# Halved modulation columns, two-group k projections, a split last output tile and a re-made order in a one-core adaLN, Hedgehog attention and MLP-mixer kernel

## The chip, the cores and the metric

The kernel runs on one core of one Trainium2 chip. The metric is the device time of one execution in microseconds (us). Three runs of the kernel before gave 551.48, 550.83 and 550.70 us, with a median of 550.83 us. One further execution was taken by the hardware profiler. It took 551.07 us, of which the span from the first instruction to the last is 549.2 us, so 1.87 us lie around the span.

## The reference, cut to what matters

The input is one sequence of 2048 rows and 512 features. A condition vector `c` gives six modulation rows, of which the change touches the first two (`sa` and `ca`).

```python
mod = (silu(c) @ w_mod).reshape(1, 6, 1, -1)
sa, ca, ga, sb, cb, gb = (mod[:, i] for i in range(6))
h = layernorm(x) * (1 + ca) + sa
x = x + ga * A(h)          # Hedgehog linear attention, 32 heads of 16
h = layernorm(x) * (1 + cb) + sb
x = x + gb * B(h)          # spatial shift mixer, then an MLP of width 1376

# A: q, k, v = h @ wqkv ; pq, pk = q @ w_phi, k @ w_phi (per head)
#    phi = concat(softmax(p), softmax(-p)) ; kv = phi_k^T v ; z = sum(phi_k)
#    o = (phi_q kv) / (phi_q z + 1e-6) ; A = o @ wo
# B: x1 = x + shift(gelu(layernorm(x) @ w1)) @ w2
#    B = x1 + gelu(layernorm(x1) @ w3) @ w4
```

## The kernel before, in words

The 2048 rows are 16 tiles of 128 rows, in 8 chunks of two tiles. Nearly every product is made of three fp32r matmuls (high and low parts of both operands), which `three` lists.

**The start.** `load_folded` multiplies the k weight (and later the q weight) by the block-diagonal `w_phi`: four groups of four matmuls each, tile names `bd`, `rk` in and `pp` out, split into high and low parts `w` by ScalarE and VectorE. `mod_cols` (L526) makes the first two modulation rows as columns. Four loads of 512 KB, one for each 128 rows of `w_mod`, bring the `sa` and `ca` columns of all 512 features. Four groups of matmuls add into one PSUM tile (32 partitions for each quarter). A copy `mod`, two transposes and two small additions then make the columns `const`. `h_chunk` turns the normalised tiles (`xn`) by transposes into `pt`, scales them with the columns, and splits them into `hh`, in two halves of two feature blocks each.

**The first pass.** For each chunk, `k_feat` and `q_feat` make the projections of k and q (12 matmuls of 512 columns in a tile `pp`), and VectorE, ScalarE and GpSimd do the two softmaxes on tiles `ke` and `qe`. `v_feat` makes v, and `kv_add` sums the products into `kva`. `zacc` sums the k features on VectorE or GpSimd. The last tile's features are not added there. They are added by matmuls (`BIAS["zpe"]`), which wait for the `ke` of tile 15.

**The later passes.** `phase_a` makes the attention output and the mixer. `up` and `down_steps` make the MLP in seven Strassen-like products of halves. `down_steps` sums each chunk of two tiles in four PSUM tiles `ac` (called `acc[0]` to `acc[3]`). `finish_rows` adds them to the residual rows `xb` by way of `uu`, and stores the result. For the last chunk, each tile's sum is added and stored in two halves of 256 columns.

**What sets the order.** Nothing is issued where it is written. Every operation is recorded in a `Plan`, and the table `ORDER` at the top of the file lists the numbers of the operations in the sequence in which they are emitted. A letter behind a number (A, V or G) moves an operation to ScalarE, VectorE or GpSimd where it has that choice. The table `SLOT` says which buffer, or which of the 8 PSUM banks, each tile uses. Each engine then runs its own instructions strictly in that order, and waits for what they need. All loads and stores go through SyncE (SP), except two small loads by ScalarE (L449). The helpers record everything, so that L468 is every matmul, L477 every transpose, L398 and L407 the copies and scalings, L415 and L417 additions on VectorE and GpSimd, L439 reductions, L445 loads and L452 stores.

Of the kernel before, what the change touches and what calls it, by code (L numbers as in the profile page):

```python
# [160 lines left out]
)  # L161
SLOT = {
    "pp": "2112103775712644371760105367611260725752737061505556300230174572340654633645407076250504027663340302"
          "145552521507",
    "bd": "13",
    "w": "174625cd387165ad28cb09",
    "rk2": "5846",
    "x2": "9",
    "st": "1377h22bbb1155hh02hg88gbf79d90221",
    "mv": "0bh0e42j01f3f380d28hebh03dg0bc0bb",  # L170
# [1251 lines left out]
```

## Time and profile before

| What | Value |
|---|---|
| Median of three runs | 550.83 us |
| Profiled execution | 551.07 us |
| Span of the profiled execution | 549.2 us |
| TensorE busy (PE) | 541.0 us, 98% |
| VectorE busy (DVE) | 492.2 us, 90% |
| GpSimd busy (POOL) | 372.7 us, 68% |
| ScalarE busy (ACT) | 339.8 us, 62% |
| Mean granted TensorE clock | 0.998 |

PE is the matmuls and PEld the weight loads that run beside them. A row of the timeline gives the start in us from the span's start, the duration in us, the engine, the line, the operation, the tiles written and read, the shape, the count, and in brackets how long the engine was idle before and what ended that. A "q" behind an engine marks its queue, which issues transfers. A row of the DMA view ends with the KB of one transfer and the us from its issue to its landing.

### The profile page before, as it was taken

What the parts mean: (1) busy time and instruction counts of PE and PEld (TensorE: products, weight loads), DVE (VectorE), ACT (ScalarE), POOL (GpSimd) and SP (SyncE); (2) the same over time, 40 slices, a digit from 0 to 9 for tenths busy, and PEclk for the clock granted to TensorE, in tenths of its full rate; (3) what the DMA queues carried; (4) which work ended last, traced back from release to release, by engine and by line L of the source; (5) the groups of instructions that cost most, each with busy time, mean ns of one, the idle gap of its engine ahead of it and who ended that gap; (6) DMA issues with size and microseconds to landing.
All of it is one profiled execution on the core that took longest, in us unless ns stands there. A gap on an engine that the chain in (4) does not pass through costs nothing.

```text
span 549.2 us, 12264 instructions
## 1 busy us (share of the span) xinstructions
PE 541.0 (98%) x4474; PEld 484.0 (88%) x4474; DVE 492.2 (90%) x899; ACT 339.8 (62%) x800; POOL 372.7 (68%) x383
## 2 busy tenths in 40 slices
PE   7999999999999999999999999999999999999997
PEld 6888788888677887888889999999999999999996
DVE  4999999999999999999998988988889768988887
ACT  2799988734436896959898576873533535234430
POOL 2388988979599999998995264433655653355354
PEclk9999999999999999999999999999999999999999
DMA  8975364247485669886898899989469746592032
GB/s 320 350 242 211 109 186 157 77 140 235 135 225 183 194 205 296 253 271 233 234 309 315 274 351 328 361 329 326 192 184 389 245 174 237 191 356 87 1 117 76
DMA packets 63668, 124.89 MB, mean 227 GB/s; under 512 B 7060, under 2 KB 26772, under 8 KB 59512
## 3 DMA queue, kind: packets, MB, share of 16 engines
q1 hardware_dynamic: 63320, 124.04, 66.4%
q8 instruction: 35, 0.57, 0.5%
q14 instruction: 25, 0.20, 0.1%
q10 hardware_dynamic: 288, 0.07, 0.1%
HBM read 89.74 MB, written 34.35 MB: 226 GB/s over the span
## 4 chain that ended last, share of the span: by engine, by line
PE 84%; DVE 9%; DMA 2%; issue 2%; POOL 2%; ACT 1%; DVEq 0%; POOLq 0%
PE pp L468 32%; PE pa L468 28%; PE ac L468 20%; PE pt L477 3%; DVE q L439 2%; DMA mod<-in_wmod 1%; DVE k L439 1%; DVE pz L439 1%; DVE pT L688 1%; DVE ke L415 1%; DMA const<-in_c 1%; DVE qe L415 1%; POOL qe L417 1%; PE kva L468 1%; ACT n L398 0%
## 5 line engine op out<-in xcount | busy, mean ns | idle before, releaser
L468 PE MATMUL pp<-w,hh 128*128 128x512 f32 x576 | 138.2, 397 | 0.0
L468 PEld LDWEIGHTS pp<-w,hh 128*128 128x128 f32 x576 | 106.8, 188 | 25.3 <-issue 1.0
L468 PE MATMUL pa<-bH,wq 128*128 128x256 f32 x840 | 105.9, 281 | 0.0
L468 PE MATMUL ac<-w,gg 128*128 128x256 f32 x840 | 105.4, 281 | 0.0
L468 PEld LDWEIGHTS ac<-w,gg 128*128 128x128 f32 x840 | 102.9, 188 | 1.2
L468 PEld LDWEIGHTS pa<-bH,wq 128*128 128x128 f32 x840 | 102.7, 188 | 0.6
L417 POOL TENSOR_TENSOR gg<-cu,gg 128x128 fp32r<-128x128 f32 (+1 forms) x32 | 21.4, 675 | 40.7 <-PE ac L468 13.8
L468 PE MATMUL pp<-w,sh 128*128 128x512 f32 x192 | 47.9, 397 | 0.0
L468 PE MATMUL pp<-w,oT 128*128 128x512 f32 x192 | 47.1, 395 | 0.0
L468 PE MATMUL pa<-nT,w 128*128 128x256 f32 x384 | 46.2, 279 | 0.0
L468 PEld LDWEIGHTS pa<-nT,w 128*128 128x128 f32 x384 | 45.1, 188 | 0.9 <-ACT mv L592 0.2
L468 PEld LDWEIGHTS pp<-w,sh 128*128 128x128 f32 x192 | 35.1, 188 | 8.6 <-POOL sh L1050 0.5
L468 PEld LDWEIGHTS pp<-w,oT 128*128 128x128 f32 x192 | 35.6, 188 | 8.0
L585 POOL TENSOR_TENSOR rs<-mv,const 128x2 f32<-128x2 f32 x31 | 24.3, 785 | 24.5 <-ACT mv L592 22.9
L398 ACT ACTIVATE cu<-pa 128x512 f32<-128x512 f32 (+1 forms) x41 | 21.3, 525 | 31.0 <-PE pa L468 13.6
L398 ACT ACTIVATE gg<-cu 128x256 fp32r<-128x256 f32 (+1 forms) x48 | 16.5, 360 | 25.0 <-PE ac L468 22.4
L417 POOL TENSOR_TENSOR e<-e,q 128x1024 f32<-128x1024 f32 x15 | 29.9, 2009 | 0.0
L415 DVE TENSOR_TENSOR gg<-sg,gg 128x512 fp32r<-128x512 f32 x36 | 26.3, 736 | 4.0 <-ACT gg L398 2.7
L417 POOL TENSOR_TENSOR ez<-e,const 128x1024 f32<-128x1024 f32 x12 | 28.8, 2407 | 0.1
L417 POOL TENSOR_TENSOR ke<-ke,k 128x1024 f32<-128x1024 f32 x14 | 28.6, 2049 | 0.0
L398 ACT ACTIVATE gg<-sg 128x512 fp32r<-128x512 f32 x28 | 17.3, 625 | 18.1 <-DVE gg L407 6.7
L415 DVE TENSOR_TENSOR cu<-pa,cu 128x512 f32<-128x512 f32 (+1 forms) x36 | 21.0, 594 | 7.5 <-PE pa L468 5.9
(221 smaller groups left out, 1224.7 us busy)
## 6 DMA issues: line engine op xcount, KB each, us to landing
wq<-dram SPq DMA_DIRECT2D x32, 1024.0 KB, 7.3
dram<-ws SPq DMA_DIRECT2D x35, 256.0 KB, 3.9
dram<-qe SPq DMA_DIRECT2D x16, 512.0 KB, 3.5
e<-dram SPq DMA_DIRECT2D x64, 128.0 KB, 3.6
xl<-in_x SPq DMA_DIRECT2D x30, 256.0 KB, 3.9
raw<-in_w SPq DMA_DIRECT2D x18, 256.0 KB, 4.0
mod<-in_wmod SPq DMA_DIRECT2D x16, 256.0 KB, 4.9
dram<-xl SPq DMA_DIRECT2D x16, 256.0 KB, 3.8
```

What stands on the lines that cost most here:

```text
L398: nc.scalar.activation(o(), i(), func, **kw)
L415: dve = ("DVE", 71 + 1.04 * o.n + 90 * (isps(a) and isps(b)), lambda: nc.vector.tensor_tensor(o(), a(), b(), op=op))
L417: pool = ("Pool", cost, lambda: nc.gpsimd.tensor_tensor(o(), a(), b(), op=op))
L439: plan.op("DVE", 65 + 1.04 * a.n + 110 * isps(o), lambda: nc.vector.tensor_reduce(o(), a(), axis=AX.X, op=op), [o], [a])
L468: nc.tensor.matmul(o(), a(), b(), start=s, stop=e, **kw)
L477: nc.tensor.transpose(o(), i(), ident())
L585: plan.op("Pool", 540 + 10 * m, lambda: nc.gpsimd.tensor_tensor(r(), v(), mhalf[:, :m](), op=OP.pow), [r], [v, mhalf])
L688: plan.op("DVE", 71 + 1.04 * o.n, lambda: nc.vector.transpose(o(), i()), [o], [i])
```

## The change

**Columns in two parts.** `mod_cols` takes a part. Part 0 makes the columns of the first 256 features (for `sa` and `ca` together), part 1 those of the other 256. The host lays the first 1024 columns of `w_mod` out anew, so that one part's columns lie together. There are still four loads of 512 KB, now two for each part, each with two blocks of 128 rows and runs of 2 KB in place of 4 KB. A load's matmuls become 8 of 128 columns in place of 4 of 256. Each part has its own copy, one transpose, and two additions.

**k of tiles 0 and 1 in two groups.** `k_feat` of chunk 0 records its 12 matmuls as two operations of 6, the first of which needs only the first half of `hh`.

**The last tile.** For the last tile's second half, `down_steps` puts the product of the remaining 96 hidden units (tile `gl`) into a PSUM tile of its own (`apart_`), and the first half's into `acc[3]`: 6 matmuls of 256 columns in place of 3 of 512. `finish_rows` adds and stores the two halves from the two tiles. The first half's store is issued by ScalarE.

**The tables.** `ORDER` and `SLOT` are replaced as a whole. The rows of these tables tell nothing by themselves. The two halves of the table `pp` below only show the kind of thing that changes.

```diff
-    "pp": "2112103775712644371760105367611260725752737061505556300230174572340654633645407076250504027663340302"
+    "pp": "1711324063347164027171451064250123635713170533160754233252706645706753646036434077762560040275463453"
...
-    def mod_cols():
+    wide = T("const", [P, NK, 32])
+    def mod_cols(part):
-        p, r, pc = T("pp", [P, HD]), T("mod", [P, HD]), T("pp", [P, 2, P])
-        for k in range(NK):
+        if part == 0:
+            act(wide, sv[:, :, None].bc([P, NK, 32]), alts=("DVE",))
+        p, r, pc = T("pp", [P, P]), T("mod", [P, P]), T("pp", [P, P])
+        for a in range(0, NK, 2):
             raw = T("mod2", [P, 2, D])
-            load(raw, wmod_d[k * P:(k + 1) * P, :2 * D].rearrange("p (j n) -> p j n", j=2), 2 * P * D * 4)
-            mms([(p[32 * (2 * j + h):32 * (2 * j + h + 1)], wide[:, k, :], raw[:, j, h * HD:(h + 1) * HD], k == 0, k == NK - 1)
-                 for j in range(2) for h in range(2)], [p], [wide, raw], skip=True, tiles=4)
+            load(raw, wmod_d[a * P:(a + 2) * P, part * D:(part + 1) * D].rearrange("(a p) n -> p a n", a=2), 2 * P * D * 4)
+            mms([(p[32 * i:32 * (i + 1)], wide[:, a + k, :], raw[:, k, i * P:(i + 1) * P], a + k == 0, a + k == NK - 1)
+                 for k in range(2) for i in range(NK)], [p], [wide, raw], skip=True, tiles=4)
         act(r, p, alts=("DVE",))
-        transp([(pc[:, i, :], r[:, i * P:(i + 1) * P]) for i in range(2)], [pc], [r])
+        transp([(pc, r)], [pc], [r])
...
-        ks = [k_feat(hh, t, wk, c * TPC + t) for t in range(TPC)]
+        ks = [k_feat(hh, t, wk, c * TPC + t, 1 if c else 2) for t in range(TPC)]
...
+        apart_ = T("ac", [P, HD]) if c == NC - 1 else None
...
+                    if t and apart_ is not None:
+                        for o, n, whole in ((apart_, slice(HD, D), True), (acc[3][:, 0, :], slice(HD), False)):
+                            mms(three(o, g[:n9, 0, sl], g[:n9, 1, sl], last["w4"][0][:n9, n], last["w4"][1][:n9, n], whole, whole),
+                                [o], [g, *last["w4"]], skip=True)
+                        continue
...
-                tt(x1[:, a, :], x1[:, a, :], p[:, a, :], OP.add)
-                store(out[rows_, a * HD:(a + 1) * HD], x1[:, a, :], P * HD * 4)
+                tt(x1[:, a, :], x1[:, a, :], apart_ if t and a else p[:, a, :], OP.add)
+                if t and not a:
+                    plan.op("Activation", 60, lambda dst=out[rows_, :HD], i=x1[:, 0, :]: nc.scalar.dma_start(dst, i()), [], [x1[:, 0, :]],
+                            land=2400)
+                else:
+                    store(out[rows_, a * HD:(a + 1) * HD], x1[:, a, :], P * HD * 4)
```

The new tables move instructions on every engine. Three places matter for what follows: the start (on two engines), the sum of the k features, and the end. In the listings a tile's number only tells it from others of its name.

**SyncE's first loads.** This is the queue of the loads at the very start, before: `rk` are the k weights (first two) and the q weights (last two), `x` is chunk 0, `xl` are later tiles, `mod` the modulation weights.

```order
L445 DMA rk_3_69<-in_wqk_t 128x2x512
L445 DMA const_78<-in_cst 128x256
L445 DMA x_7_80<-in_x 128x2x512
L445 DMA rk_8_82<-in_wqk_t 128x2x512
L445 DMA mod_9_84<-in_wmod 128x1024
L445 DMA mod_11_91<-in_wmod 128x1024
L445 DMA mod_12_93<-in_wmod 128x1024
L445 DMA mod_14_100<-in_wmod 128x1024
L445 DMA rk_16_104<-in_wqk_t 128x2x512
L445 DMA rk_18_108<-in_wqk_t 128x2x512
L445 DMA xl_119<-in_x 128x512
```

The same queue after the change, up to the last of the two parts' loads:

```order
L445 DMA const_69<-in_cst 128x256
L445 DMA rk_5_76<-in_wqk_t 128x2x512
L445 DMA rk_6_78<-in_wqk_t 128x2x512
L445 DMA xl_80<-in_x 128x512
L445 DMA x_8_82<-in_x 128x2x512
L445 DMA rk_10_89<-in_wqk_t 128x2x512
L445 DMA xl_91<-in_x 128x512
L445 DMA rk_12_93<-in_wqk_t 128x2x512
L445 DMA mod_14_97<-in_wmod 128x2x512
L445 DMA mod_17_106<-in_wmod 128x2x512
L445 DMA mod_27_142<-in_wmod 128x2x512
L445 DMA mod_29_146<-in_wmod 128x2x512
```

The two q weight loads and two tiles of chunk 1 now stand ahead of the modulation weights.

**VectorE from the columns to the first k.** Before, the columns are the two additions into `const_224` (one row, x2), and all of `hh` follows them:

```order
L407 TENSOR_SCALAR mod_219<-pp_183 128x256
L426 TENSOR_SCALAR const_224<-pp_221 128x2x2 x2
L407 TENSOR_SCALAR pt_214<-pt_214,const_224 128x256
L407 TENSOR_SCALAR pt_202<-pt_202,const_224 128x256
L407 TENSOR_SCALAR hh_243<-pt_202 128x512
L415 TENSOR_TENSOR hh_243<-pt_214,hh_243 128x512
L415 TENSOR_TENSOR hh_243<-pt_202,hh_243 128x512
L415 TENSOR_TENSOR w_271<-pp_238,w_254 128x4x128
```

After, `const_270` is written twice, for the first 256 features and then for the others, and the two halves of `hh` lie around the second:

```order
L426 TENSOR_SCALAR const_270<-pp_261 128x2 x2
L407 TENSOR_SCALAR w_210<-pp_213 128x4x128
L415 TENSOR_TENSOR w_246<-pp_213,w_210 128x4x128
L415 TENSOR_TENSOR hh_293<-pt_263,hh_293 128x512
L426 TENSOR_SCALAR const_270<-pp_316 128x2 x2
L407 TENSOR_SCALAR pt_252<-pt_252,const_270 128x256 x2
L407 TENSOR_SCALAR hh_293<-pt_252 128x512
L415 TENSOR_TENSOR hh_293<-pt_252,hh_293 128x512
L407 TENSOR_SCALAR w_210<-pp_205 128x4x128
L415 TENSOR_TENSOR w_246<-pp_205,w_210 128x4x128
```

The folds of the q weights (`w_210`, `w_246`) moved in between. On TensorE, all eight groups of folds now stand ahead of the modulation matmuls, the eight transposes of chunk 1 stand between the two parts, and the k matmuls come behind part 1's transpose: 6 of tile 1, 12 of tile 0, and the other 6 of tile 1.

**TensorE at the sum of the k features.** Late in the first pass, two rows (`pp` from `za`, then from `ke`) sum the k features of all tiles by matmuls with ones. `ke` is tile 15, still to be finished by VectorE. Before, they stand behind 36 matmuls of 512 columns that follow a group of `kva`:

```order
L468 MATMUL pp_1756<-w_351,hh_1193 128x512
L468 MATMUL pp_1756<-w_288,hh_1193 128x512
L468 MATMUL pp_1777<-za_825,const_67 32x256 x4
L468 MATMUL pp_1777<-ke_1720,const_67 32x256 x4
L468 MATMUL pp_1796<-w_288,hh_1398 128x512
```

After, with the same `kva` group ahead:

```order
L468 MATMUL pp_1800<-w_358,hh_1374 128x512
L468 MATMUL pp_1800<-w_352,hh_1374 128x512
L468 MATMUL pp_1817<-za_856,const_67 32x256 x4
L468 MATMUL pp_1817<-ke_1704,const_67 32x256 x4
L468 MATMUL pp_1835<-w_352,hh_1374 128x512
```

Now 48 matmuls of 512 columns stand between that `kva` group and the sum: one projection of 12 has moved ahead of it.

**VectorE at the end.** These are the last instructions of VectorE before. `ac_7381`, `ac_7392`, `ac_7404` and `ac_7447` are the last chunk's `acc[0]` to `acc[3]`, `xb_6790` and `xb_7365` its two tiles of rows.

```order
L415 TENSOR_TENSOR xb_6790<-xb_6790,ac_7381 128x256
L415 TENSOR_TENSOR xb_6776<-xb_6776,ac_7279 128x512
L407 TENSOR_SCALAR uu_7500<-ac_7381 128x256
L415 TENSOR_TENSOR gg_7437<-cu_6863,gg_7363 128x256
L415 TENSOR_TENSOR uu_7500<-uu_7500,ac_7381 128x256
L415 TENSOR_TENSOR uu_7500<-uu_7500,ac_7392 128x256
L415 TENSOR_TENSOR xb_7365<-xb_7365,xc_7357 128x512
L415 TENSOR_TENSOR xb_7365<-xb_7365,ac_7392 128x256
L415 TENSOR_TENSOR uu_7500<-uu_7500,ac_7392 128x256
L415 TENSOR_TENSOR xb_6790<-xb_6790,ac_7404 128x256 x2
L415 TENSOR_TENSOR xb_7365<-xb_7365,ac_7447 128x256 x2
```

After, `acc[0]` to `acc[3]` are `ac_7447`, `ac_7398`, `ac_7418` and `ac_7549`, and `apart_` is `ac_7544`:

```order
L407 TENSOR_SCALAR uu_7510<-ac_7447 128x256
L415 TENSOR_TENSOR xb_6765<-xb_6765,ac_7315 128x512
L415 TENSOR_TENSOR uu_7510<-uu_7510,ac_7447 128x256
L415 TENSOR_TENSOR xb_7378<-xb_7378,xc_7368 128x512
L415 TENSOR_TENSOR uu_7510<-uu_7510,ac_7398 128x256
L415 TENSOR_TENSOR xb_7378<-xb_7378,ac_7398 128x256
L415 TENSOR_TENSOR uu_7510<-uu_7510,ac_7398 128x256
L415 TENSOR_TENSOR xb_6795<-xb_6795,ac_7447 128x256
L415 TENSOR_TENSOR xb_6795<-xb_6795,ac_7418 128x256 x2
L415 TENSOR_TENSOR xb_7378<-xb_7378,ac_7544 128x256
L415 TENSOR_TENSOR xb_7378<-xb_7378,ac_7549 128x256
```

The last two rows now read two tiles, and the addition of `acc[0]` to the first tile's rows moved from the first row shown to the row ahead of `ac_7418`. In the new `SLOT` table `acc[3]` has the bank of `acc[0]`, and `apart_` that of `acc[1]`; before, the four had a bank each. So the matmuls into `apart_` wait for the last read of `acc[1]`, and those into `acc[3]` for the last read of `acc[0]`.

More of the change, by code (lines that the diff above doesn't have):

```diff
@@ L40 @@
 ORDER = (
[120 rows of a table removed]
[120 rows of a table added]
 )
 SLOT = {
-    "pp": "2112103775712644371760105367611260725752737061505556300230174572340654633645407076250504027663340302"
[L164 to L170, printed above, removed]
-    "rs": "29812hcbbjji851d0ie93863874jh6213",
-    "nm": "3fa4a54dde4e1jjcf2883583gaacj278gb331h60ed7ha0092e635b5a",
-    "xn": "10cg751eba368fe9",
@@ L174 @@
-    "mod": "lh9g7ejf9i4638bkia",
-    "mod2": "0213",
+    "pp": "1711324063347164027171451064250123635713170533160754233252706645706753646036434077762560040275463453"
+          "62046562621057",
+    "bd": "2j",
+    "w": "134702cd89516a7d49c210",
+    "rk2": "4195",
+    "x2": "3",
+    "st": "201e1g254426a5555ca22555f27582006",
+    "mv": "4355172614f1f5a4hac5dic53c22cccg0",
+    "rs": "9232251141c55d5ab5a1fed21a4e82084",
+    "nm": "6402c757j74f422161488a44dd699b5jjijj2fc8b5i7fc1ehge226d2",
@@ L176 @@
+    "xn": "f083kge1k95hlici",
+    "mod": "i9805j174ejdf793i1g",
+    "mod2": "2647",
     "kva": "4",
     "za": "7",
-    "hh": "30a89be0",
-    "pt": "06254521753213317025344576360400",
-    "raw": "da1k0d63f6hg40cljd4940abi353",
-    "k1": "2430035525435132",
-    "ke": "4501639451823940",
-    "k2": "1213035252034134",
-    "vv": "ib4j953cdj19a75f",
-    "qe": "3792232883214942",
-    "q1": "2440243225135053",
-    "qt": "5e97g70fkccg",
-    "xl": "abd42002jf51cl836e2i1h3b0j5g2je53k0hhej4hlahd0",
@@ L189 @@
-    "acc": "cl8hi",
-    "kvs": "f",
-    "pz": "1",
-    "q2": "10141003",
-    "e": "5617956758034928",
-    "ez": "8348813999970750",
-    "q3": "2212223043334222",
-    "q5": "23253203",
-    "pT": "4272394975373487",
-    "oT": "99594b24",
-    "nT": "9999bb2e",
-    "n": "1931gfgfahafb63g",
-    "h": "7kd9l62c7i1lfkcd",
-    "gf": "17555662",
-    "sh": "2520ecb0",
-    "pa": "762553462761040036271541705740316243253470661263027034160772",
-    "wr": "80061",
-    "ws": "khe217da8lk4eba05bb5dfgfd71i652ak90",
@@ L207 @@
-    "gb": "8",
-    "tw": "98935",
-    "bL": "47604149",
-    "nb": "1ahb5c79egg4jc3f",
-    "yt": "e5jkbdh7j9l9a6cd",
-    "bH": "52804219431594595069127578657523",
-    "tr": "714eb039akdl4172",
-    "wq": "490c934e174e3174e7314e7134ee3417e431",
-    "cu": "672egi14f3fl25b7c10g4hg9ked6l14g9cd0jblf",
-    "gl": "c3jca56i",
-    "ac": "26311567160267423016415376013542",
-    "gg": "32781952372584716531287609873295063284107962583012103241806937415809263740821596",
-    "sg": "bkbka76k6hk6h4kj6a25j37b2lbji26k2i2594k2",
@@ L220 @@
-    "xb": "9had9ei0fc3ha71e",
-    "xc": "5lj03023672l0gfh",
-    "uu": "j3347ell",
+    "hh": "86596bea",
+    "pt": "05266253756236307563344627135340",
+    "raw": "akl5db94201k385ljd4940abi353",
+    "k1": "0231523433000413",
+    "ke": "4506239453821940",
+    "k2": "3112123212413411",
+    "vv": "bf4c218453gde20k",
+    "qe": "2798812825711992",
+    "q1": "1243144314035413",
+    "qt": "hfe58k5d0h08",
+    "xl": "k4hd6282blae03h76e2i3e5b0jjg2jeb3k0hhej9hlahd3",
+    "acc": "6c4gh",
+    "kvs": "d",
@@ new lines @@
+    "pz": "1",
+    "q2": "12313230",
+    "e": "5637986458013928",
+    "ez": "1841273373970050",
+    "q3": "0001000001142121",
+    "q5": "14233433",
+    "pT": "1553393927171752",
+    "oT": "47ee0744",
+    "nT": "ab744343",
+    "n": "fbb787g7daafb63g",
+    "h": "gkd9l62c7i1lfkcd",
+    "gf": "73510949",
+    "sh": "0abe2b2e",
+    "pa": "572553547504540036271543705740316243053470661263027010166772",
+    "wr": "10064",
+    "ws": "0j629gdfe9lab6a15fcf3fghdh1i652ak90",
+    "gb": "8",
+    "tw": "93534",
@@ new lines @@
+    "bL": "07600143",
+    "nb": "1ahb5a794eg4j5ab",
+    "yt": "eg6kbdhej9lj20cd",
+    "bH": "82865219931451257925167078517526",
+    "tr": "710ek536g42l010l",
+    "wq": "30ec03b85e5b38e5be38be583beeb583e5b8",
+    "cu": "672egi14fkfl25b7c10g4hg9ked6l14g9cd0jblf",
+    "gl": "c3jca5e5",
+    "ac": "263115671602674206354153760125325",
+    "gg": "32781452832481796237489625863492354180697320581769960241803976415809234760821593",
+    "sg": "bkb6f76keh96h4kj6a2ja37b27lji26k2i2296i2",
+    "xb": "9had9ei0fc3ha71k",
@@ L223 @@
+    "xc": "0lj030j3i42bl45f",
+    "uu": "j33jakll",
 }
@@ L524, in mod_acc @@
         return acc
-    def mod_cols():
-        wide = T("const", [P, NK, 32])
-        act(wide, sv[:, :, None].bc([P, NK, 32]), alts=("DVE",))
-        p, r, pc = T("pp", [P, HD]), T("mod", [P, HD]), T("pp", [P, 2, P])
-        for k in range(NK):
+    wide = T("const", [P, NK, 32])
[4 more added lines that the diff above has]
+        for a in range(0, NK, 2):
             raw = T("mod2", [P, 2, D])
-            load(raw, wmod_d[k * P:(k + 1) * P, :2 * D].rearrange("p (j n) -> p j n", j=2), 2 * P * D * 4)
-            mms([(p[32 * (2 * j + h):32 * (2 * j + h + 1)], wide[:, k, :], raw[:, j, h * HD:(h + 1) * HD], k == 0, k == NK - 1)
-                 for j in range(2) for h in range(2)], [p], [wide, raw], skip=True, tiles=4)
+            load(raw, wmod_d[a * P:(a + 2) * P, part * D:(part + 1) * D].rearrange("(a p) n -> p a n", a=2), 2 * P * D * 4)
+            mms([(p[32 * i:32 * (i + 1)], wide[:, a + k, :], raw[:, k, i * P:(i + 1) * P], a + k == 0, a + k == NK - 1)
+                 for k in range(2) for i in range(NK)], [p], [wide, raw], skip=True, tiles=4)
         act(r, p, alts=("DVE",))
-        transp([(pc[:, i, :], r[:, i * P:(i + 1) * P]) for i in range(2)], [pc], [r])
+        transp([(pc, r)], [pc], [r])
         for j in range(2):
-            ts(cols[:, j, :].re("p (h i) -> p h i", (2, 2), h=2).perm("p h i -> p i h", (1, 0)), pc[:, :, 64 * j:64 * (j + 1):32],
-               float(j), None, OP.add, None)
+            ts(cols[:, j, 2 * part:2 * part + 2], pc[:, 64 * j:64 * (j + 1):32], float(j), None, OP.add, None)
     mods = T("dram", [NK, D])
@@ L682, in body @@
     plan.at("mod")
-    mod_cols()
+    mod_cols(0)
+    plan.at("mod_")
+    mod_cols(1)
     sa, ca1 = cols[:, 0, :], cols[:, 1, :]
@@ L779, in softmax_in, with k_feat @@
             act(heads2(e)[:, :, i, :], heads2(e)[:, :, i, :], AF.Exp, scale=1.0 - 2.0 * i)
-    def k_feat(hh, t, w, tt_):
+    def k_feat(hh, t, w, tt_, parts=1):
         plan.at(f"k{tt_}")
         mm, e = T("k1", [P, 2, H]), T("ke", [P, 2 * D])
-        p = proj(rows(hh, t), w, mm, e)
+        p = proj(rows(hh, t), w, mm, e, parts=parts)
         marks["k"] = marks["proj"]
@@ L1334, in down_steps, with finish_rows @@
                 marks["down"] = done
-                finish_rows(c, acc)
+                finish_rows(c, acc, apart_)
             yield
-    def finish_rows(c, acc):
+    def finish_rows(c, acc, apart_):
         xs = []
@@ L1407 @@
         "in_c": a["c"].reshape(NK, P).T,
-        "in_wmod": a["w_mod"],
+        "in_wmod": np.concatenate([a["w_mod"][:, :2 * D].reshape(D, 2, 2, HD).transpose(0, 2, 1, 3).reshape(D, 2 * D), a["w_mod"][:, 2 * D:]], 1),
         "in_id": np.eye(P, dtype=np.float32),
```

240 rows, old and new, of the table ORDER are left out of this document.

## The prediction

> **What bounds the kernel now.** I read the page first: the share of each engine, and the chain that ended last.
>
> ```profile
> span 549.2 us, 12264 instructions
> PE 541.0 (98%) x4474; PEld 484.0 (88%) x4474; DVE 492.2 (90%) x899; ACT 339.8 (62%) x800; POOL 372.7 (68%) x383
> PE 84%; DVE 9%; DMA 2%; issue 2%; POOL 2%; ACT 1%; DVEq 0%; POOLq 0%
> ```
>
> TensorE (PE) is busy all but 8.2 us, and the chain lies on it for 84%. The change takes no matmul column away, so it can gain only in those 8.2 us, or where PE is busy with work that could have been done earlier. The table by stage shows where they lie.
>
> ```profile
> 0.00:10.00 10.00, 7.21 (x44) 6.86 (x45) 3.26 (x15) 1.63 (x3) 2.14 (x9) 1.00 0.81 288
> 10.00:20.00 10.00, 9.80 (x93) 7.60 (x92) 8.55 (x19) 5.37 (x13) 1.69 (x4) 1.00 1.05 394
> 40.00:60.00 20.00, 20.00 (x87) 16.13 (x87) 19.93 (x28) 19.80 (x48) 17.87 (x16) 1.00 0.51 181
> 100.00:150.00 50.00, 48.98 (x523) 38.72 (x522) 48.22 (x58) 24.02 (x47) 39.96 (x27) 1.00 0.43 135
> 400.00:500.00 100.00, 100.00 (x831) 99.21 (x831) 84.72 (x187) 39.22 (x87) 47.94 (x65) 1.00 0.72 256
> 540.00:549.20 9.20, 5.44 (x41) 4.97 (x39) 5.16 (x14) 0.00 (x0) 3.03 (x3) 0.91 0.32 114
> ```
>
> The columns are stage, length, then busy us of PE, PEld, DVE, ACT and POOL, granted clock, DMA share and GB/s. PE is idle 2.8 us in the first ten, 1.0 between 100 and 150, and 3.8 at the end; from 400 to 500 never. VectorE (DVE) is as full as PE from 40 to 60 (19.93 of 20) and nearly so from 100 to 150, so in the first pass a gain must be one for both. The timeline of PE shows the start.
>
> ```profile
> 8.70 2.92 PE L468 MATMUL pp<-bd,rk 128*128 128x128 f32 x24 [1.76 <-DMA rk<-in_wqk_t]
> 14.04 0.64 PE L468 MATMUL pp<-mod,const 128*32 128x256 f32 x8
> 15.23 0.44 PE L477 MATMUL pp<-const,mod 128*128 128x128 f32 x2
> 15.50 3.74 PE L468 MATMUL pp<-bd,rk 128*128 128x128 f32 x32
> 18.99 5.84 PE L468 MATMUL pp<-w,hh 128*128 128x512 f32 x24
> 24.68 1.03 PE L477 MATMUL pt<-const,xn 128*128 128x128 f32 x8
> 25.46 5.83 PE L468 MATMUL pp<-w,hh 128*128 128x512 f32 x24
> ```
>
> The last modulation load's matmuls run at 14.04, the folds of the q weights fill 15.50 to 18.99, k of tiles 0 and 1 starts at 18.99, chunk 1's transposes follow at 24.68, and the next projections start at 25.46. From there PE runs without a gap worth naming until 140.
>
> **The start.** Loads on SyncE's queue land one after the other, so I place the new ones by the bytes ahead of them. The rows are the issue (start first) and, from the DMA view of that moment, the us to landing.
>
> ```profile
> 4.84 0.56 SPq L445 DMA_DIRECT2D mod<-in_wmod  x1
> mod<-in_wmod SPq DMA_DIRECT2D x1, 512.0 KB, 8.9
> 5.93 0.77 SPq L445 DMA_DIRECT2D rk<-in_wqk_t  x1
> rk<-in_wqk_t SPq DMA_DIRECT2D x1, 512.0 KB, 10.5
> 6.77 0.44 SPq L445 DMA_DIRECT2D xl<-in_x  x1
> xl<-in_x SPq DMA_DIRECT2D x1, 256.0 KB, 10.3
> ```
>
> The fourth modulation load, with 3.625 MB (of 1024 x 1024 bytes) on the queue up to its end, lands at 4.84 + 8.9 = 13.7. The second q load (4.625) lands at 5.93 + 10.5 = 16.4, and the `xl` (4.875) at 17.1. That is 1.35 us for each 512 KB. In the new queue part 0 ends at 4.125 MB, hence at 15.1, and part 1 at 5.125 MB, at 17.1 + 0.7 = 17.8. So part 0 comes 1.4 us later than all columns did, and part 1 4.1 us later. Nothing is gained in the landing; what is gained is that the q folds (3.5 us of PE) and chunk 1's transposes (25.46 - 24.68 = 0.8 us) are done in the wait.
>
> The Trainium skill speaks against this (DMA: Bandwidth & Descriptors, "Where 436 GB/s comes from"): it puts the HBM limit of one core at about 358 GB/s. The row of 10 to 20 us shows 394. By the page's figure the last 1.57 MB ahead of part 1 would take 4.4 us in place of 4.0, an estimate, and the start's gain would shrink by 0.4; the measured rate decides.
>
> The steps from the columns on have these rows, in the order copy, columns, scaling, high part, low part:
>
> ```profile
> 14.75 0.42 DVE L407 TENSOR_SCALAR mod<-pp 128x256 f32<-128x256 f32 x1 [0.24 <-PE pp L468]
> 15.70 0.23 DVE L426 TENSOR_SCALAR const<-pp 128x4 f32<-128x4 f32 x2 [0.53 <-PE pp L477]
> 15.97 1.19 DVE L407 TENSOR_SCALAR pt<-pt,const 128x256 f32<-128x256 f32 x2
> 17.19 0.60 ACT L398 ACTIVATE hh<-pt 128x512 fp32r<-128x512 f32 x1
> 17.82 1.29 DVE L415 TENSOR_TENSOR hh<-pt,hh 128x512 fp32r<-128x512 f32 x2
> ```
>
> Part 0: landing 15.1, matmuls 0.64, copy at most 0.42 (half as wide), transpose 0.3, columns 0.23, scaling 1.19 and high part 0.60 give 18.5, and the low part (half of 1.29) 19.1. ScalarE has other work queued ahead of that copy, for which I add 0.2. Part 1: landing 17.8 and matmuls 0.64 give 18.4, but its copy stands on ScalarE behind the first high part (18.7). With copy and transpose PE is free for k at 19.3, against 18.99 before. The second half of `hh` then needs columns, scaling and high part, all on VectorE (0.23 + 1.19 + 0.60 = 2.0 us), so it is there at 21.4, and its low part 0.64 later. The first two groups of 6 matmuls last until 19.3 + 12 x 5.69 / 24 = 22.1. So no gap, or one up to 0.5 if those steps wait for each other. The 24 matmuls take 18.99 to 24.68 = 5.69 and end at 25.0, where the next projections follow, against 25.46. I take -0.5; bounds: +0.4 (part 1 late by 0.4, a gap of 0.5) and -0.9. The 32 modulation matmuls in place of 16 are half as wide, and cost at most another 0.64 for a load, in a wait for the next; the first operation of 6 adds no instruction.
>
> **The sum of the k features.** PE's 1.02 of idle time between 100 and 150 is the wait for tile 15.
>
> ```profile
> 138.56 2.40 DVE L415 TENSOR_TENSOR ke<-ke,k 128x1024 f32<-128x1024 f32 x1
> 141.01 0.64 PE L468 MATMUL pp<-ke,const 128*32 128x256 f32 x8 [1.02 <-DVE ke L415]
> ```
>
> The re-made order puts 12 more matmuls ahead of it: 12 x 5.69 / 24 = 2.8 us. If VectorE came to `ke` at the same time, the wait would be gone with 1.8 to spare. But VectorE, full by the row of 40 to 60, now has its columns at 19.4 rather than 15.7, 3.7 us later, with some of the folds done in between and the rest still ahead. So the wait is worth between 0 and its full 1.02: I take half, -0.5. What is late next is the attention's first product, which needs VectorE's transposes.
>
> **The end.** Here PE has stopped and the rest hangs on the last product: its last matmuls, the two additions, the two stores with their time to landing, and, for comparison, what ScalarE takes to issue a load.
>
> ```profile
> 544.22 0.86 PE L468 MATMUL ac<-w,gl 96*128 96x512 f32 x3
> 544.92 0.52 PE L468 MATMUL ac<-w,gg 128*128 128x256 f32 x3
> 545.54 0.75 DVE L415 TENSOR_TENSOR xb<-xb,ac 128x256 f32<-128x256 f32 x2 [0.99 <-PE ac L468]
> 546.42 0.38 SPq L452 DMA_DIRECT2D out_dram<-xb  x1
> out_dram<-xb SPq DMA_DIRECT2D x1, 128.0 KB, 1.8
> 0.71 0.45 ACTq L449 DMA_DIRECT2D const<-in_c  x1
> ```
>
> Before, the last store is issued at 546.42, behind both additions and the other store. After, only one half waits for the last matmul; its addition ends at about 545.96 and ScalarE, with nothing else to do (0.00 busy since 540), issues the store at once: 546.0, so -0.4. The six narrow matmuls cost what three wide ones did (544.92 - 544.22 = 0.70 for 3 x 512 columns; 15 of 256 take 1.78 from 542.44 to 544.22, so six 0.71). ScalarE's store may take 0.1 longer to issue (0.45 against 0.38).
>
> ```profile
> 541.56 0.93 DVE L415 TENSOR_TENSOR uu<-uu,ac 128x256 f32<-128x256 f32 x2
> 542.44 1.94 PE L468 MATMUL ac<-w,gg 128*128 128x256 f32 x15
> 543.47 0.41 DVE L415 TENSOR_TENSOR uu<-uu,ac 128x256 f32<-128x256 f32 x1
> 543.80 0.75 DVE L415 TENSOR_TENSOR xb<-xb,ac 128x256 f32<-128x256 f32 x2
> ```
>
> Against that, the change adds a wait: `apart_` and `acc[3]` take the banks of `acc[1]` and `acc[0]`, so PE's last 21 matmuls (2.5 us) are queued behind VectorE's last reads of those, and nobody else can go on. Between the end of `acc[1]` and `apart_` PE has 18 narrow matmuls and 3 wide ones, 18 x 0.119 + 0.70 = 2.8 us. VectorE needs four additions there (541.56 to 543.80 before: 2.24 us with one more between). If it is on time nothing is lost; if it is as late as before, when the last such read ended at 543.88 and PE was at 543.1 with `acc[3]`, PE stops for 0.8. I take 0.1: the end is worth -0.3 (bounds -0.4 and +0.5).
>
> **The sum.** -0.5 - 0.5 - 0.3 = -1.3 us on the profiled execution, 551.07 (span 549.2 and 1.87 around it), which is 0.24 over the median of the runs. On the median: 550.83 - 1.3 = 549.5 us. For the rest of the new order, from 190 us on, I put nothing: it moves hundreds of instructions, but as PE is 100.00 of 100.00 busy in 400 to 500, it cannot gain there, only lose.
>
> **The rivals.**
> (a) *VectorE takes the start's gain back.* It is as full as PE until 60 and after 100. If its list decides when the attention starts, PE waits there for what it gained, and only the end is left: 550.83 - 0.3 = 550.5. For it speaks 19.93 of 20; against it that the row of 100 to 150 leaves DVE 1.8 us of idle time, which a later start can use up.
> (b) *Both waits go wholly:* start -0.9, sum -1.02, end -0.4, in all -2.3: 548.5. For it speaks the 1.8 to spare.
> (c) *Slower: the shared banks and new waits on VectorE.* The new order makes VectorE serve the first pass 3.7 us later and PE needs its results in the same places. If `ke` or the attention's transposes come later than PE by more than the start has gained, PE stops where it did not. With VectorE 2.0 late behind its columns, less 0.5 gained at the start, plus 0.5 at the banks, it is +2.0: 552.8. It is slower than before as soon as VectorE comes to its transposes over 0.3 later than before, since only the end's gain stands against that. Against it speaks that DVE does folds in the wait for part 1 that it did later before.
> (d) *The granted clock falls.* PE now waits up to 2 us between the parts (15.7 to 17.8, less chunk 1's transposes). The row of 0 to 10 shows 1.00 with a wait of 1.76 in it, so I give it little; at half clock over the first 12 k matmuls it would cost 2.8: 552.3. The Trainium skill (TensorE: Matmul & The Clock Gate, Part 1) has PE fall to half rate after an idle window of about 3.4 us; no wait here is that long.
>
> **How the numbers follow.** Chances: the forecast 0.45, (a) 0.22, (b) 0.12, (c) 0.18, (d) 0.03. A measurement of this kernel tells about 0.2% from no change, 1.1 us, so faster is below 549.7 and slower above 551.9. The forecast's own range by its bounds is 548.5 to 551.0; three quarters of it, 0.34, is faster and 0.11 the same. With (b) faster is 0.46; with (a) the same is 0.33; (c) and (d) are slower, 0.21. The range reaches from 548.0, a little under (b), to 552.0, which leaves out (c), (d) and less than the rest of 2 in 10.
>
> **What would show it.** Right: k starts near 19.3 behind part 1's transpose, with no row of PE between 19 and 25 idle over 0.3, and the next projections start at 25.0; the wait for `ke` is under 0.6; the last store is issued by ScalarE within 0.6 us of the last matmul; PE is not idle ahead of `ac` from `gl` near the end. Wrong: the second half of `hh` comes later than 22.6; PE waits in 150 to 200 for `pT` or `oT`; PE has new idle time between 200 and 540; or the last 21 matmuls wait for VectorE by more than 0.4.

## The result, and the profile after

| | before | after |
|---|---|---|
| Median, runs beside each other | 551.15 us (4 runs, 550.70 to 551.60) | 557.79 us (4 runs, 556.85 to 558.24) |
| Profiled execution, its span | 551.07 us, 549.2 us | 558.24 us, 556.5 us |
| First k product, first q projection | 18.99, 25.46 us | 19.26, 24.92 us |
| First attention product of chunk 1 | 187.29 us | 185.66 us |
| End of the last matmul | 545.44 us | 553.17 us |

The ratio is 1.0122, interval 1.0109 to 1.0135: slower by 6.6 us, where 549.5 was forecast. The page of the changed kernel:

```profile
span 556.5 us, 12363 instructions
PE 546.0 (98%) x4509; PEld 487.3 (88%) x4509; DVE 500.1 (90%) x884; ACT 347.6 (62%) x817; POOL 372.3 (67%) x384
```

By its shares nothing has changed: PE is at 98%, VectorE at 90%. The table by stage of the changed kernel tells more (columns as in the prediction).

```profile
0.00:10.00 10.00, 8.91 (x56) 8.41 (x56) 3.25 (x12) 2.77 (x5) 1.91 (x9) 1.00 0.85 287
100.00:150.00 50.00, 50.00 (x532) 39.81 (x532) 48.71 (x60) 25.04 (x50) 41.73 (x27) 1.00 0.45 143
200.00:250.00 50.00, 48.09 (x455) 41.97 (x455) 46.40 (x78) 38.61 (x85) 46.08 (x43) 0.97 0.81 244
250.00:300.00 50.00, 46.99 (x375) 38.95 (x375) 48.63 (x78) 39.88 (x106) 41.33 (x42) 1.00 0.76 245
```

The same table of the kernel before, from 200 to 300:

```profile
200.00:250.00 50.00, 49.98 (x472) 42.65 (x471) 48.40 (x78) 37.45 (x87) 47.85 (x45) 1.00 0.90 281
250.00:300.00 50.00, 50.00 (x426) 44.00 (x425) 47.28 (x89) 45.58 (x120) 42.53 (x48) 1.00 0.83 266
```

In the first ten 1.09 us of PE's idle time are left of 2.79, and 100 to 150 has none. But 200 to 300 now has 4.9 us of it (1.91 + 3.01; before 0.02), and a clock of 0.97 in its first half. The timeline of PE in the changed kernel shows the places: the start, the sum of the k features, and the two longest new waits.

```profile
17.19 1.08 PE L468 MATMUL pp<-mod,const 128*32 128x128 f32 x32
19.26 11.41 PE L468 MATMUL pp<-w,hh 128*128 128x512 f32 x48 [0.23 <-DVE hh L415]
...
141.39 0.64 PE L468 MATMUL pp<-za,const 128*32 128x256 f32 x8
141.84 0.63 PE L468 MATMUL pp<-ke,const 128*32 128x256 f32 x8
...
185.66 1.16 PE L468 MATMUL pp<-pT,const 64*32 64x128 f32 x64
...
199.75 0.38 PE L468 MATMUL pa<-nT,w 128*128 128x256 f32 x1
202.05 7.34 PE L468 MATMUL pa<-nT,w 128*128 128x256 f32 x47 [1.91 <-DVE nT L415]
...
282.41 1.09 PE L477 MATMUL pt<-const,n 128*128 128x128 f32 x8 [1.35 <-DVE n L407]
```

k starts at 19.26, the 48 matmuls from there (24 of k, 24 of the next projections) run without a break, the `ke` row has no bracket any more (1.02 us before), and at 185.66 the kernel is 1.63 us ahead of before. Then PE waits 1.91 us for `nT`, in the middle of chunk 1's first mixer product, and its 47 remaining matmuls take 7.34 us.

**Why `nT` is late.** The timeline of VectorE in the changed kernel ahead of that wait, and then that of GpSimd:

```profile
194.79 0.23 DVE L434 SCALAR_TENSOR_TENSOR pz<-q,pz 128x64 f32<-128x64 f32 x1
194.93 3.34 DVE L415 TENSOR_TENSOR ws<-wr 128x256 f32<-128x256 f32 x1
198.20 0.28 DVE L415 TENSOR_TENSOR q<-pz,q 128x128 f32<-128x128 f32 x1
...
200.71 1.28 DVE L415 TENSOR_TENSOR nT<-pt,nT 128x512 fp32r<-128x512 f32 x2
```

```profile
193.54 2.06 POOL L417 TENSOR_TENSOR qe<-qt,q 128x1024 f32<-128x1024 f32 x1
195.52 0.13 POOL L1056 MEMSET sh<- 128x8 f32 x1
195.59 2.40 POOL L417 TENSOR_TENSOR ez<-e,const 128x1024 f32<-128x1024 f32 x1
```

One subtraction of 256 columns, a part of the preparation of `w3` (`s3 = a11 - a21` in `split_w3`), takes 3.34 us. It ends 0.28 us after GpSimd's second long multiplication (197.99). Everything behind it on VectorE is about 3 us late, the low parts of `nT` among it. Before, GpSimd did this subtraction itself, as the timeline of GpSimd in the kernel before shows:

```profile
194.80 0.75 POOL L417 TENSOR_TENSOR ws<-wr 128x256 f32<-128x256 f32 x1
```

**The clock.** Windows of the changed kernel (the granted clock stands behind the five engines):

```profile
202.00:203.00 1.00, 0.95 (x8) 0.95 (x9) 1.00 (x1) 0.99 (x2) 1.00 (x2) 1.00 1.05 298
203.00:206.00 3.00, 3.00 (x19) 3.00 (x18) 2.89 (x7) 2.32 (x6) 3.00 (x3) 0.58 0.92 225
206.00:207.00 1.00, 1.00 (x7) 1.00 (x7) 1.00 (x2) 0.97 (x4) 1.00 (x2) 0.56 0.03 8
207.00:208.00 1.00, 1.00 (x11) 1.00 (x10) 1.00 (x2) 1.00 (x4) 1.00 (x2) 1.00 0.57 213
```

From 203.46 on, 1.4 us behind the end of the wait, PE is at half rate for 3.41 us, until 206.87. That costs 1.7 us, and is why 47 matmuls took 7.34 us.

### The profile page after: what moved, and what is told of

Its sections match the earlier page's. It is cut to its first block, busy times and chain, and to the rows that moved or that the text cites. A ratio compares the mean times of both kernels' runs of the same rounds, so it can differ in the third digit from the quotient of the medians.

```text
span 556.5 us, 12363 instructions
## 1 busy us (share of the span) xinstructions
PE 546.0 (98%) x4509; PEld 487.3 (88%) x4509; DVE 500.1 (90%) x884; ACT 347.6 (62%) x817; POOL 372.3 (67%) x384
## 4 chain that ended last, share of the span: by engine, by line
PE 49%; DVE 6%; issue 2%; POOL 2%; ACT 0%; DVEq 0%; POOLq 0%
PE pa L468 22%; PE ac L468 20%; PE pp L468 6%; DVE pT L691 1%; DVE pz L439 1%; DVE pp L434 1%; DVE q L439 1%; DVE h L415 0%; DVE h L434 0%; POOL ez L417 0%; DVE ez L415 0%; POOL ws L417 0%; POOL rs L586 0%; PE pt L477 0%; DVE nT L415 0%
## 5 line engine op out<-in xcount | busy, mean ns | idle before, releaser
L468 PE MATMUL pa<-nT,w 128*128 128x256 f32 x384 | 49.9, 288 | 2.2 <-DVE nT L415 1.9
L468 PEld LDWEIGHTS pa<-nT,w 128*128 128x128 f32 x384 | 48.1, 194 | 3.9 <-DVE nT L415 2.5
L417 POOL TENSOR_TENSOR gg<-cu,gg 128x256 fp32r<-128x256 f32 (+1 forms) x28 | 19.1, 687 | 40.3 <-PE pa L468 14.9
L398 ACT ACTIVATE gg<-cu 128x256 fp32r<-128x256 f32 (+1 forms) x53 | 18.2, 357 | 29.7 <-PE ac L468 16.8
L586 POOL TENSOR_TENSOR rs<-mv,const 128x2 f32<-128x2 f32 x31 | 22.5, 726 | 21.3 <-ACT mv L593 19.8
L398 ACT ACTIVATE gg<-sg 128x512 fp32r<-128x512 f32 x31 | 19.2, 625 | 28.1 <-DVE sg L415 20.4
L398 ACT ACTIVATE cu<-pa 128x512 f32<-128x512 f32 (+1 forms) x38 | 19.1, 523 | 23.9 <-PE pa L468 19.9
L417 POOL TENSOR_TENSOR w<-raw,w 128x512 fp32r<-128x512 f32 (+3 forms) x21 | 25.6, 1221 | 9.3 <-ACT w L398 9.2
```

What stands on the lines that cost most here:

```text
L398: nc.scalar.activation(o(), i(), func, **kw)
L417: pool = ("Pool", cost, lambda: nc.gpsimd.tensor_tensor(o(), a(), b(), op=op))
L468: nc.tensor.matmul(o(), a(), b(), start=s, stop=e, **kw)
L586: plan.op("Pool", 540 + 10 * m, lambda: nc.gpsimd.tensor_tensor(r(), v(), mhalf[:, :m](), op=OP.pow), [r], [v, mhalf])
```

## The experiments

Theory A: two operations that the new tables put on VectorE were held there while GpSimd worked through its own, and that made PE wait. B: VectorE is too full in the new order as a whole. C: it is the added work, wherever it stands. D: the edits themselves cost the time. Where only `ORDER` was edited, the diff shows the neighbouring words (a word is one operation's number with its letter). In experiments 4 and 6 to 9 the new order stands up to a seam and the old order behind it; there `SLOT` was made anew as well, and in experiment 10 its row `ac`. Line numbers in the kernels of experiments 1 to 10 are 6 lower.

**1. The subtraction back on GpSimd.**

```diff
-844 1016 848 986 860 1017 1121G
+844 1016 848 986G 860 1017 1121G
```

> The changed kernel with one letter altered: the subtraction that makes s3 of chunk 2's w3 split (ws<-wr, 128x256, VectorE, 3.34 us at 194.93 in the changed kernel's trace, 0.75 us on GpSimd before) goes back to GpSimd. Theory A (this subtraction was held on VectorE until GpSimd's row of multiplications ended, and delayed nT): the wait of 1.9 us at 202 us is gone, the granted clock is 1.00 in 200 to 210, the second block of pa<-nT takes about 6 us in place of 7.3, and the time falls by 3 to 4 us, to about 554.3. Theory B (the new order spends VectorE's slack everywhere, so another operation is late next): a wait of like size appears within 20 us, and the time stays within 0.8 us of 557.8.

554.65 us, ratio 1.0072 (1.0058 to 1.0086). The timeline of PE and the window of 200 to 210 in this kernel:

```profile
199.48 5.82 PE L462 MATMUL pa<-nT,w 128*128 128x256 f32 x48
```

```profile
200.00:210.00 10.00, 10.00 (x124) 8.83 (x124) 9.89 (x17) 9.27 (x21) 9.92 (x9) 1.00 1.03 299
```

No wait, full clock, 3.1 us less from one letter. A holds here, and B fell for this wait. The time is still 3.6 us over that of before.

**2. The same subtraction on VectorE, at another place.** Its copy (996, ScalarE) moves with it.

```diff
-848 986 860 1017 1121G 845 1018 690 1116 849 996 925 691 846 1222 1019 850 675 1020 926
+848 860 1017 1121G 845 1018 690 1116 849 925 691 846 1222 1019 850 675 1020 986 996 926
```

> The changed kernel with the same subtraction left on VectorE, but placed six VectorE operations later, behind the last small product of chunk 3's denominators; its copy on ScalarE is placed behind it. VectorE's work is the same in sum. Theory A: by then GpSimd's long multiplication is at its end, the subtraction takes under 1 us, the copies and subtractions of nT are done by about 199.7, the wait at 202 is under 0.3 us, and the time is about 554.3. A rival (C: it is the extra work on VectorE, wherever it stands, that makes nT late): the wait stays near 1.9 us and the time near 557.8.

554.81 us (1.0055 to 1.0082), like the first. VectorE and GpSimd in this kernel:

```profile
198.19 0.52 DVE L409 TENSOR_TENSOR ws<-wr 128x256 f32<-128x256 f32 x1
```

```profile
195.97 2.46 POOL L411 TENSOR_TENSOR ez<-e,const 128x1024 f32<-128x1024 f32 x1
```

It comes 0.24 us before GpSimd's multiplication ends, and takes 0.52. VectorE's work is the same as in the changed kernel, so C fell.

**3. The kernel before, with only this subtraction on VectorE.**

```diff
-527 917 980G 836
+527 917 980 836
```

> The kernel before with one letter altered: the same subtraction (0.75 us on GpSimd at 194.80) goes to VectorE. Theory A: GpSimd then runs without a gap to about 199.2, the subtraction takes 3 us or more on VectorE, nT comes 3 us later, TensorE waits 1 to 4 us near 201 to 204, and the time is 552.5 to 555.5. Theories B and C: VectorE has 0.4 us more, and the time is within 0.6 us of 551.1.

553.56 us, ratio 1.0046 (1.0030 to 1.0062). VectorE, GpSimd and PE in this kernel:

```profile
194.20 2.47 DVE L409 TENSOR_TENSOR ws<-wr 128x256 f32<-128x256 f32 x1
```

```profile
193.67 0.72 POOL L579 TENSOR_TENSOR rs<-mv,const 128x2 f32<-128x2 f32 x1
194.33 2.05 POOL L411 TENSOR_TENSOR qe<-qt,q 128x1024 f32<-128x1024 f32 x1
```

```profile
202.50 3.68 PE L462 MATMUL pa<-nT,w 128*128 128x256 f32 x30 [1.98 <-DVE nT L409]
```

One letter makes the same wait in the old order: A holds. The operation took 2.47 us, not the "3 us or more" expected, because GpSimd soon had nothing left to do: its next multiplication waited for VectorE.

**4. The edits with the old order from chunk 0 on.** `ORDER` is the changed kernel's for its first 178 words; behind them come the other operations in the order of before (renumbered), with the new last stores.

```diff
-103 171 339 132 340 342 104 134G
+103 171 217 213 114 73 216G 104
```

> All three edits of the change (columns in two parts, k of two tiles in two groups, last tile in two banks), with the new order only up to chunk 0's k products, and from there on the order of the kernel before. Theory A (the new order of the middle costs the time, the edits do not): no wait in 190 to 300 over 0.3 us, the end about 0.4 us shorter than before, the start 0 to 0.5 us later, 550.3 to 551.5. Theory D (the edits themselves cost the time, for example by the 64 matmuls of 128 columns or the shared banks): 553 or more.

552.65 us (1.0018 to 1.0041): between both. No wait came back in 190 to 300 (PE 99.97 of 100 in 200 to 300). But the seam cost: PE waited 0.6 us for `hh` and 0.2 for `ke` in 20 to 100, and 0.6 for an `rk` load ahead of them. A run in which the seam adds waits neither clears nor convicts the edits; the sixth to ninth clear them.

**5. The second held operation to ScalarE.** The first experiment's kernel, and:

```diff
-1498 1277 1273V 1401
+1498 1277 1273 1401
```

> The changed kernel with the subtraction of the first experiment on GpSimd, and the normalization of tile 10 (n<-h, 128x512, VectorE, 2.72 us at 279.64 in the changed kernel's trace, where others of its form take 0.76) on ScalarE, which ran it in the kernel before. Theory A (it too was held on VectorE by GpSimd's row of operations, and everything behind it on VectorE came 2 us later): the wait of 1.35 us at 282 goes, the wait of 0.67 us at 297 shrinks too, and the time falls from 554.65 to 552.3 to 553.4. Theory B (VectorE is simply too full in 260 to 300): the waits move on, and the time stays above 554.

In the changed kernel it looked like this, first VectorE, then GpSimd:

```profile
279.64 2.72 DVE L407 TENSOR_SCALAR n<-h,rs,nm 128x512 f32<-128x512 f32 x1
```

```profile
278.97 0.75 POOL L417 TENSOR_TENSOR ws<-wr 128x256 f32<-128x256 f32 x1
279.67 2.40 POOL L417 TENSOR_TENSOR w<-tw,w 128x1024 fp32r<-128x1024 f32 x1
```

With it on ScalarE: 551.85 us, ratio 1.0019 (1.0010 to 1.0028), 2.8 us less than the first, more than expected. The waits at 282 and 297 are both gone; the windows of this kernel:

```profile
200.00:250.00 50.00, 49.91 (x470) 42.95 (x469) 47.26 (x75) 39.74 (x89) 47.01 (x46) 1.00 0.87 268
250.00:300.00 50.00, 49.30 (x407) 42.28 (x407) 47.71 (x84) 44.47 (x117) 45.05 (x47) 1.00 0.82 252
```

By the medians, two words of 2800 were 5.9 of the 6.6 us. The kernel is still slower than before by 0.19%, though it has the new start, the new sum and the new end.

**6. New order to 190 us, old order behind.** As in the fourth, but the first 908 words, up to the one ahead of the subtraction.

```diff
-844 1016 848 986 860 1017 1121G
+844 1016 675 1037 860 690 986G
```

> All three edits; the new order up to the word ahead of the slow subtraction (about 190 us), and from there on the order of the kernel before, with the end of the new one. Theory A: the 1.3 us by which the changed kernel leads at 185 us and the 0.4 us of its end stay, less what the seam costs: 549.2 to 550.6, faster than both kernels. If the first stages of the new order cost time too (as the 552.65 of the run with the old order from chunk 0 on could mean): 551 to 553.

551.21 us, ratio 1.0009 (1.0000 to 1.0018). It misses 549.2 to 550.6 because ScalarE's list at the seam was late: PE waited 1.84 us at 197.25 for `n`. With that wait in it the kernel is at the time of before, so D fell. But nor was the gain seen.

**7. The seam 13 us later.** 946 words, the subtraction on GpSimd.

```diff
-935 676G 764 856 765 1022 997G
+935 676G 1037 991G 764 1022 992
```

> All three edits; the new order up to about 203 us with the subtraction of the first experiment on GpSimd, and from there on the order of the kernel before, with the end of the new one. The seam lies behind the place at which the sixth experiment waited 1.84 us. Theory A: the waits in 190 to 540 sum to under 0.5 us, and what the start, the k features and the end gained is left: 549.0 to 550.0, faster than both kernels. If the seam costs as much as in the sixth experiment: 550.8 to 551.5.

550.48 us, ratio 0.9993 (0.9984 to 1.0002): no difference that can be told, short of the 549.0 to 550.0 expected. In its profiled execution PE waited 1.37 us at 291 for `n` from ScalarE, which had stood 2.3 us for a load.

**8. That load 4 us earlier.** The seventh's kernel, with the load (1779) directly behind the one ahead of it.

```diff
-1268 1780 1559
+1268 1780 1779 1559
...
-1093G 1779 1335
+1093G 1335
```

> The kernel of the seventh experiment (new order with the subtraction on GpSimd up to about 203 us, old order behind) with one load moved: the second mixer load of rows of chunk 2 (256 KB, issued at 276.94 there and landed 7.6 us later at 284.50, among the loads of turned rows) stands directly behind the first, 4 us earlier on SyncE's queue. If that load's lateness makes the wait of 1.37 us at 291 (ScalarE stood for 2.3 us ahead of it): the wait is under 0.3 us and the median falls from 550.48 to 549.2 to 550.0. If the wait hangs on something else, such as VectorE's order: 550.2 to 550.8.

550.56 us, ratio 0.9991 (0.9982 to 1.0000). The wait at 291 is gone and so are the longest runs (549.89 to 550.96, against 549.84 to 551.69), but the median stayed: the mechanism was right, the expected gain not.

**9. The seam where it costs least.** 1256 words, with the edits of experiments 1 and 8.

```diff
-1082 1249 1492 1250 1389 1257 1493G
+1082 1249 1389 1190 1257 1483G 1216
```

> All three edits; the new order with the subtraction on GpSimd up to about 255 us, the old order behind, with the load of the eighth experiment moved in the same way. At this seam only 3 operations of the new order stand earlier than in the old one (22 at the seam of the seventh experiment), so the seam itself should cost nothing. If the lead of 1.6 us at 185 us was lost at the seams so far: 549.2 to 550.2. If the new order loses it in 200 to 260 even without the held subtraction (its waits there in the first experiment sum to 0.8 us): 550.3 to 551.3.

550.71 us, ratio 0.9999 (0.9990 to 1.0008): the second case. It shows where the gain goes. The first attention products of chunk 1 and chunk 3, first in this kernel, then in the kernel before:

```profile
185.86 1.16 PE L462 MATMUL pp<-pT,const 64*32 64x128 f32 x64
264.02 1.16 PE L462 MATMUL pp<-pT,const 64*32 64x128 f32 x64
```

```profile
187.29 1.16 PE L468 MATMUL pp<-pT,const 64*32 64x128 f32 x64
263.94 1.16 PE L468 MATMUL pp<-pT,const 64*32 64x128 f32 x64
```

1.43 us ahead at 186, 0.08 behind at 264. Between the two rows both kernels run the same matmuls, so the lead is lost there, without one long wait (the longest is 0.27 us).

**10. Only the last tile's edit, on the kernel before.** `down_steps` and `finish_rows` as in the change, and the old order with the second half's product and addition ahead.

```diff
+    apart_ = T("ac", [P, HD]) if c == NC - 1 else None
...
-                finish_rows(c, acc)
+                finish_rows(c, acc, apart_)
```

> The kernel before with only the edit of the last tile (its second half's product in a bank of its own, its first half's store issued by ScalarE). By the forecast's own term the end is 0.3 us shorter (0 to 0.4): 550.6 to 551.1. Against it: 6 matmuls of 256 columns in place of 3 of 512 cost 0.35 us of TensorE and the end gains nothing: 551.1 to 551.5.

550.58 us, ratio 0.9993 (0.9984 to 1.0002): 0.34 less in the medians, as the term of the forecast said, within what can't be told from none. In the profiled execution the time from the end of the last matmul to the end is 3.43 us, against 3.77 before.

**11. The disputed cost by itself.** A kernel of its own, in one execution; two of its lines:

```diff
+nc.gpsimd.tensor_tensor(go, ga, gb, op=OP.mult)  # 14 times
+nc.vector.tensor_tensor(o[:, :256], a[:, :256], b[:, :256], op=OP.subtract)  # 8 times
```

> Not the model's computation but the disputed cost by itself, the output being one tile repeated. GpSimd runs three trains of 14 multiplications (128x1024, about 2.1 us each) with no pause. Beside each, VectorE runs 8 operations of one form, each followed by a reduction of one SBUF tile (about 0.6 us): subtractions 128x256 with both inputs in SBUF, then with one input in PSUM, then TENSOR_SCALAR 128x512 from SBUF to SBUF. Theory A: the first form takes 1.5 to 4 us each (0.38 alone), as it waits until GpSimd's operation, or the next one too, is over; the second form takes 0.38 each and the reductions 0.6. The third form, which was 2.72 us once in the changed kernel, is held too. Against it (VectorE was slow for another reason, such as its own queue or the loads): all forms take their usual time.

The groups of VectorE's instructions (mean ns behind the busy us); the eight subtractions of the first form ran behind each other, the reductions later:

```profile
L48 DVE TENSOR_TENSOR o<-a,b 128x256 f32<-128x256 f32 x8 | 16.4, 2052 | 0.2
L45 DVE TENSOR_REDUCE q<-a 128x16 f32<-128x512 f32 x24 | 16.4, 681 | 0.6
L54 DVE TENSOR_SCALAR o<-a,s 128x512 f32<-128x512 f32 x8 | 12.9, 1609 | 0.1
L51 DVE TENSOR_TENSOR o<-psum,b 128x256 f32<-128x256 f32 x8 | 3.3, 417 | 0.1
```

The same subtraction takes 2052 ns in the mean with both inputs in SBUF (six of the eight took 2.44 to 2.45 us, the other two 1.32 and 0.42), and 417 with one in PSUM. TENSOR_SCALAR from SBUF to SBUF is held (1609; the last two, after GpSimd's train, took 0.55 us), the reduction is not. So it is neither VectorE's queue nor the loads. This agrees with the Trainium skill (SBUF — State Buffer, "Who interferes with whom"): a VectorE instruction with two SBUF inputs, or in a mode with two ports, and a GpSimd instruction that reads SBUF exclude each other, whoever starts first blocks the other to the end of its instruction, and a reduction takes no part in it.

## Why the prediction was wrong

**The start: the number is right, the gain isn't shown.** k is at 19.26 (forecast 19.3), no wait over 0.23 stands behind it, and the next projections are at 24.92 (25.0) against 25.46: -0.54 for -0.5. But that compares one execution with one. In the profiled runs of experiments 3 and 10, which have the old start, these projections begin at 24.98 and 25.04; in the nine with the new start they begin at 24.84 to 26.11. PE waited 0.6 to 1.2 us for one of the first loads in experiments 2, 4, 5, 8 and 9, as it had waited 1.76 us in the profile of before. The means are 25.16 with the old start and 25.26 with the new one, so the agreement was luck.

**The sum of the k features: gone wholly, in part for another reason.** It is -1.02 for -0.5. The 12 matmuls ahead of it are there, but VectorE did not come to `ke` at the same time: it came at 140.48 instead of 138.56, 1.9 us later, and took 1.21 us instead of the 2.40 in the prediction's own row. The multiplication has two inputs in SBUF. Before, GpSimd was busy from 136.22 to 139.87 as it ran; after, GpSimd was idle beside it. So the wait of 1.02 in the kernel before looks itself like the price of a held operation, 2.40 - 1.21 = 1.19 us long. The row was on the page and was taken for the operation's usual time.

**The end: right.** 553.17 to 556.46 is 3.29 us, before 545.44 to 549.21 is 3.77: -0.5 for -0.3. In the other kernels with the new end it is 3.28 to 3.47. Its lines in the changed kernel:

```profile
552.65 0.52 PE L468 MATMUL ac<-w,gg 128*128 128x256 f32 x3
553.21 0.42 DVE L415 TENSOR_TENSOR xb<-xb,ac 128x256 f32<-128x256 f32 x1 [1.24 <-PE ac L468]
553.71 0.35 ACTq L1378 DMA_DIRECT2D out_dram<-xb  x1
```

ScalarE's store follows 0.54 us after the last matmul, and PE did not wait for the shared banks.

**Wrong: "For the rest of the new order, from 190 us on, I put nothing".** The same sentence says that it "cannot gain there, only lose", and then prices the loss at zero. From chunk 1's attention product to the last matmul the changed kernel lost 1.63 + 7.73 = 9.4 us. The brackets of the new waits are 4.9 in 200 to 300, but a wait costs more than its bracket, as a matmul's row ends later than the next could have started. At the wait for `nT` two matmuls start 2.30 us apart (199.75 and 202.05), where 48 of them take 5.82 us in experiment 1, 0.12 each: it cost 2.18 us, not 1.91. Counted in this way the nine waits of over 0.1 us behind 190 cost 6.9, and the half clock 1.7. The remaining 0.8 is spread in slightly longer rows of PE and isn't settled.

The two held operations are not the whole of it. With both put back (experiment 5) the first attention product of chunk 1 starts at 187.01, 0.28 ahead of before, and the last matmul ends at 548.04, 2.60 behind: 2.9 us are still lost from there on. Nor did a held operation have to come from another engine. `ez<-e,const` took 1.22 us on VectorE before, at 243.63 and at 248.70; in the changed kernel it takes 1.76 at 249.30 and 1.96 at 252.36, and in experiment 5 and experiment 9 the same 1.76 and 1.96, with other operations of GpSimd beside it. That is 1.3 us of VectorE in the stretch in which experiment 9 loses its lead. No run here tests whether it is the cause.

The range was also summed up too narrowly. Its bounds are +0.4 for the start, 0 for the sum and +0.5 for the end, which gives 551.7 and not 551.0; and the -0.9 for the start is worked out nowhere. Neither would have reached 557.79.

**The rivals.** (c) had the right sign and named VectorE, but looked for its lateness ahead of 190 and at the banks, and priced it at 2.0. (a) (VectorE takes the gain back) was not needed in the first pass, where VectorE kept up, but describes experiment 9: from 190 to 265 the other engines take the lead back. Why is argued, not shown: GpSimd was busy 50.00 of 50 us in 150 to 200 before the change, and 50.00 in experiment 9. (d) looked at the start alone, and was discarded because no wait was as long as 3.4 us; a wait of 1.9 was enough.

**How it could have been seen.** The order after the change was there to read, engine by engine. Of the operations that came to VectorE from another engine only six run between 140 and 300 us: `ws<-wr` (194.9), `sh<-gf,sh` (271.0), two `xl<-pp` (288.1, 295.5) and two `n<-h` (279.6, 297.1). The two `xl` read PSUM. Of the other four, two were held and took 3.34 and 2.72 us; the `sh` (0.68) and the second `n` (0.77) were not. GpSimd's row at the first place in the trace of before (busy 50.00 of 50 in 150 to 200) was the warning.

## What to carry to other kernels

In a kernel whose order is a table, look first at the operations that change engine, and for each that comes to VectorE with its inputs in SBUF, at what GpSimd is running then. Its price is its own time plus the rest of GpSimd's instruction, and here in three cases of four the whole next instruction as well. Then look at the operations that stay on VectorE and get other neighbours on GpSimd. A row of VectorE that takes twice the time of its form is a sign of this, before a change as after it. A stage without idle time is no reason to price a new order there at nothing; it has only losses to offer, so it needs a bound of its own. A lead won early is worth only what the engines that serve the later stages can follow.
